# Attention with a state and top-1 experts on one Trainium2 core: first loads moved to SyncE's queue, idle products ahead of the first batch, batch 2 turned earlier, the last result stored sooner

## The chip, the cores and the metric

The kernel runs on one core of a Trainium2 chip. The metric is the device time of one execution in microseconds, the median of three runs. Besides it there is a profile of one execution: for each engine (TensorE or PE, its weight loads PEld, VectorE or DVE, ScalarE or ACT, GpSimd or POOL, and SyncE or SP, which only issues transfers) every instruction with its start and its duration. The span of the profile is the time between the first and the last instruction of the execution.

## What is computed

Two blocks, one behind the other, in float32. The first is an attention between tokens x, (8, 8, 512, 64) for batch, head, token and width, and 32 states per batch and head, in both directions. The second sends every one of the 8 x 544 rows of 512 numbers that come out to one of eight experts, the one with the largest logit.

```
scores  = softmax(0.125 * x @ state^T);  xread = scores @ state     # 512 rows per batch and head
scores2 = softmax(0.125 * state @ x^T);  sread = scores2 @ x        # 32 rows per batch and head
rows    = concat(xread, sread), heads side by side                  # (8*544, 512)
e       = argmax(rows @ w_gate);  gate = softmax(rows @ w_gate)[e]
out     = gate * (relu(rows @ w1[e]) @ w2[e])                       # w1[e] 512x1024, w2[e] 1024x512
```

## The kernel before

The 512 token rows of a batch nearly always want the same expert, so each batch is run through one expert, whose number is found from the data. The 256 rows that come from the states are sorted by expert into groups of 32 and run four groups at a time, in "rounds" of 128 rows; each row group streams its own expert's weights. Three rounds are run in the main path.

**Batches.** For batch b, `states_w1` multiplies the states by w1 once (PSUM `pG`, copied to `G`), so that the first expert layer becomes `up`: for each of eight f, one product of `G` with the attention weights `aT` (`aTe` or `aTl` in the profile) into `ph`, and a relu by ScalarE into `hT`. The second layer is `down` for batches 0 to 2 (products `py`, results `y`) and `down_by_halves` for batches 3 to 7. The latter replaces eight block products by seven (`pX`, `pD`, `pX`, `pY`, `pZ`, `pW`, `pD`, in this order), with sums made by VectorE (`Sa`, `Sb`) and GpSimd (`Ta`, `Tb`); its four results `yC`, `yD`, `yB`, `yA` (`yh` in the profile) are stored from ScalarE's queue, `yA` after the last `pD`.

**Attention.** `stages(b)` is a generator: each of its steps runs in one slot. The first step turns x (`xt`, two VectorE transposes) and the states (`stT`: a VectorE transpose into 64 partitions, and a copy to the other 64 by the engine passed in). Later steps make scores (`pc`), their transposes `sx`, the exponentials, `aT` and, for the other direction, the weights `a`, their transposes `pt` and rows `pw`, then logits (`pl`), counts (`pr`) and the choice of the expert (`eb`), which SyncE reads to address the expert's weights.

**Order.** All compute instructions keep the order in which the program writes them (the wrapper `InOrder`). Work is interleaved by hand: `up`, `down` and `down_by_halves` call `next(insert)` between products, and each call is one slot: it runs a step of `others()`, which is first the attention of later batches, then `sort_states`, then the rounds. A generator's bare `yield` lets a slot pass. Batch 0 and part of batch 1 have no earlier batch to hide beside: `begin()` writes them out, first with `up` of half of batch 0's rows (`one`), then of the other half (`two`) with steps of `beside()` between them. `first()` takes batch 1 to its end.

**Rounds.** `round_x` transposes the 128 rows (`ptx`, evicted to `sxT`), `round_up` multiplies by w1 (`pgh`), `round_h` transposes the hidden rows (`pth`), `round_down` multiplies by w2 (`pgy`) and `round_out` scales the result (`ys`, VectorE) and stores it with an indirect transfer from GpSimd. The weight tiles of the rounds (`s` in the profile, 1 MB each in four transfers of 256 KB) have S1B = 4 and S2B = 3 buffers, and `fetch` asks for the next one after each use; all of them, like the batches' weights `w1t` and `w2t`, go through SyncE's queue in the order of the program. Each transfer also waits for the one issued eight transfers before it.

PSUM has four banks in the pool `ps_p` (the function `bank`), four for `pc` while the attention lasts, and later two for `ps_t` and two for `ps_g`. In the profile, nearly all instructions have line 48, that of the wrapper, so groups are told apart by their tiles.

Of the kernel before, what the change touches and what calls it, by code (L numbers as in the profile page):

```python
# [20 lines left out]
def kernel(  # L21
# [46 lines left out]
    NFC = F // 128  # L68
# [24 lines left out]
    def load_x(b, q):  # L93
        x_nat[b] = att.tile([128, H, NC, D], FP32, tag="x", bufs=3, name="x_nat")
        for h in (slice(0, 4), slice(4, 8)):
            q.dma_start(out=x_nat[b][:, h].rearrange("p h c d -> p h (c d)"),
                        in_=x[b, h].rearrange("h (p c) d -> p h (c d)", c=NC))
# [3 lines left out]
    def load_states(b, q0, q1):  # L101

        rows = state[b].rearrange("h n d -> n h d")
        to = st2[b] = att.tile([64, H, D], FP32, tag="st", bufs=3, name="st2")
        q0.dma_start(out=to[0:32], in_=rows)
        for u in range(2):
            q1.dma_start(out=to[32:64, :, ts(u, 32)], in_=rows[:, :, ts(1 - u, 32)])
# [89 lines left out]
    def bank(name):  # L197
        return ps_p.tile([128, 512], FP32, tag="p", name=name)
# [3 lines left out]
    def turn_x(b, xt, h):  # L202
        dve.transpose(xt[:, h].rearrange("p h c u t -> p (h c u t)"),
                      x_nat[b][:, h].rearrange("p h c d -> p (h c d)"))
# [107 lines left out]
    def fetch_batch(b):  # L312
        if b < B:
            load_x(b, sp)
            load_states(b, sp, sp)
# [116 lines left out]
    def begin():  # L432

        nonlocal G, hT

        ps = bank("pss")[:, 0:4]
        for q in range(4):
            pe.matmul(ps[:, q:q + 1], lhsT=st2[0][0:32].rearrange("n h d -> n (h d)").rearrange("n (p c) -> n c p", c=4)[:, q, :],
                      rhs=ones_f[0:32], start=True, stop=True, skip_group_check=True)
        sums = att.tile([128, 4], FP32, name="sums")  # L440
        dve.tensor_copy(out=sums[:], in_=ps)
        pr = bank("prg")[0:1, 0:E]
        for q in range(4):
            pe.matmul(pr, lhsT=sums[:, q:q + 1], rhs=wg4[:, q, :], start=(q == 0), stop=(q == 3), skip_group_check=True)
        most(0, pr)
        turn_states(0, act.copy)
        xt, sx = new_xt(), new_sx()
        turn_x(0, xt, slice(0, 4))
        e = expert_of(eb, 0)
        at_once(w1_parts(0, e, 2))  # L450
        turn_x(0, xt, slice(4, 8))
        pc = new_pc()
        for g in range(2):
            scores(0, xt, pc, g)
        one, two = slice(0, 2), slice(2, 4)
        soft[0] = (sx,)
        turn_scores(pc, sx, 0)
        turn_scores(pc, sx, 1)
        less_max(sx, one, dve)
        exponential(sx, one)  # L460
        load_x(1, act)
        act.dma_start(out=wg[:], in_=moe_w_gate.rearrange("(c p) e -> p c e", p=128))
        load_states(1, act, act)
        turn_scores(pc, sx, 2)
        turn_scores(pc, sx, 3)
        over_sum(sx, one, dve)
        turn_read(0, one)
        G = states_w1(new_G(), w1s[0], stG[:, 0])
        less_max(sx, two, dve)
        exponential(sx, two)  # L470
        nm = write_max(pc)
        over_sum(sx, two, dve)
        turn_read(0, two)
        at_once(w2_parts(0, e))
        fetch_batch(2)
        for r in range(NR):
            sp.dma_start(out=ss_dram[ts(r, 128)], in_=blank[:])
        hT = new_hT()
        up(G, aT[0], hT, one)
        soft[0] += write_weights(pc, nm)  # L480
        xt, sx = new_xt(), new_sx()
        turn_x(1, xt, slice(0, 4))
        turn_x(1, xt, slice(4, 8))
        turn_states(1, act.copy)
        first_e = att.tile([1, 1], FP32, name="first_e")
        dve.tensor_copy(out=first_e[:], in_=eb[0:1, 0:1])

        def beside():
            for b in range(2):
                states_gates(b)  # L490
            pc = new_pc()
            scores(1, xt, pc, 0)
            yield

            pr = bank("pre")[:, 0:1]
            pe.matmul(pr, lhsT=ones_f[0:1].to_broadcast([1, 128]), rhs=first_e[:], start=True, stop=True)
            scores(1, xt, pc, 1)
            exps, gates = logits_x(0)
            dve.tensor_copy(out=eb[:, 0:1], in_=pr)
            for i in range(4):  # L500
                turn_scores(pc, sx, i)
            less_max(sx, ALL, dve)
            nm = write_max(pc)
            yield
            exps()
            gates()
            count(0)
            turn_write(0)
            yield
            write_rows(0)  # L510
            exponential(sx, ALL)
            soft[1] = (sx,) + write_weights(pc, nm)
            over_sum(sx, ALL, dve)
            turn_read(1)
            yield
        up(G, aT[0], hT, two, beside())

# [8 lines left out]
    def w1_parts(b, e, cols=1):  # L526

        t = w1s[b] = wpool.tile([128, NDC, F], FP32, tag="w1", name="w1t")
        rows = moe_w1[ds(e, 1)].rearrange("o (c p) f -> p (o c) f", p=128)
        f = F // cols  # L530
        return [lambda k=k: sp.dma_start(out=t[:, :, ts(k, f)], in_=rows[:, :, ts(k, f)]) for k in range(cols)] if cols > 1 else \
            [lambda k=k: sp.dma_start(out=t[:, k], in_=rows[:, k]) for k in range(NDC)]
# [6 lines left out]
    def at_once(parts):  # L539
        for p in parts:  # L540
            p()
# [9 lines left out]
    def new_G():  # L551
        return ffn.tile([128, 2, F], FP32, tag="G", name="G")

    def states_w1(G, w1t, st, halves=(0, 1), bank=bank):

        for k in halves:
            pg = [bank("pG") for _ in range(2)]
            for q in range(4):
                for g in range(2):
                    pe.matmul(pg[g][ts(q, 32), :], lhsT=st[ts(g, 64), q, :],  # L560
                              rhs=w1t[ts(g, 64), q, ts(k, 512)], start=True, stop=True, skip_group_check=True)
            for g in range(2):
                act.copy(G[:, g, ts(k, 512)], pg[g][:])
        return G
# [299 lines left out]
    def rounds(r0, r1):  # L864
        need1.extend((r, k, half) for r in range(r0, r1) for k in range(NDC) for half in range(2))
        need2.extend((r, f) for r in range(r0, r1) for f in range(NFC))
        round_experts(r0)
        fetch(2, 0)
        yield
        yield  # L870
        round_in(r0)
        fetch(S1B - 2, S2B)
        for _ in range(5):
            yield
        for r in range(r0, r1):
            round_x(r)
            if r + 1 < r1:
                round_experts(r + 1)
                round_in(r + 1)
            yield  # L880
            for k in range(NDC):
                round_up(r, k)
                fetch(2, 0)
                yield
                if k < NDC - 1 and r + 1 < r1:
                    yield
            round_relu(r)
            yield
            round_h(r)
            yield  # L890
            for f in range(0, NFC, 2):
                for i in range(2):
                    round_down(r, f + i)
                    fetch(0, 1)
                yield
                if r + 1 < r1 or f < 2:
                    yield
            round_out(r)


    begin()

    def first():

        yield
        turn_write(1)
        exps, gates = logits_x(1)
        yield
        exps()
        choose(1)  # L910
        e1 = expert_of(eb, 1)
        at_once(w1_parts(1, e1))
        lazy.extend(w2_parts(1, e1))
        gates()
        yield
        write_rows(1)
        yield
        xsT = [turn_rows(b) for b in range(2)]
        yield
        for b in range(2):  # L920
            logits_s(b, xsT[b])

    lazy = []

    def attention():

        gens, slot = [first()], 0
        while gens:
            b = 2 + slot // 4
            new = slot % 4 == 0 and b < B  # L930
            if new:
                gens.append(stages(b))
                next(gens[-1])
            for g in gens[:len(gens) - new]:
                try:
                    next(g)
                except StopIteration:
                    gens.remove(g)
            slot += 1
            yield  # L940
# [170 lines left out]
```

## Time and profile before

| | |
|---|---|
| time | 468.24 us (467.53 to 468.88, three runs) |
| profiled execution | 467.59 us, span 465.8 us |
| first TensorE product of batch 0's scores | 8.93 us |
| first product of `up`, batch 0 | 18.72 us |
| first `pg` product of batch 2 | 52.41 us |
| `pG` of batch 1 | 72.34 us |
| last TensorE product ends | 459.15 us |
| `yA` stored, issue by ScalarE | 460.10 us |
| `ys` of the last round stored, issue by GpSimd | 461.00 us |
| HBM read and written | 94.15 MB and 14.95 MB |

A line of the timeline gives the start, the duration, the engine, the source line, the operation with its tiles as out<-in, the shape and the number of instructions merged into it; in brackets stands the idle time of that engine just before, and what ended it. "issue" is time in which the engine waited for nothing that the profile shows: its sequencer was busy issuing something else. A table of windows gives, for each stretch of time, how long each engine was busy in it, the clock that TensorE was granted as a share of full speed (PEclk), the share of time the DMA engines were busy and what they moved.

### The profile page before, as it was taken

To read this page: it belongs to the slowest core of one execution; us is meant where nothing else is said; L and a number is where in the kernel's file an instruction comes from. 1 tells how busy PE (TensorE), PEld (TensorE's weight loads), DVE (VectorE), ACT (ScalarE), POOL (GpSimd) and SP (SyncE) were. 2 spreads that over 40 slices of the span, in tenths; PEclk is the share of its full clock that TensorE was granted. 3 is DMA by queue.
4 is the path that set the end of the run, shared out by engine and by line. 5 is a ranking of instruction groups with operands and counts; after the bars stand their busy time and mean duration, and the time that the engine had idled before them with its cause. 6 is when DMAs were issued, how large, how long until landed. Compare 5 with 4: busy or idle time off the path is not lost. (4 is left out here: it accounts for less than half of the span.)

```text
span 465.8 us, 9496 instructions
## 1 busy us (share of the span) xinstructions
PE 441.5 (95%) x3699; PEld 252.8 (54%) x3699; DVE 178.0 (38%) x445; ACT 120.0 (26%) x267; POOL 87.1 (19%) x75
## 2 busy tenths in 40 slices
PE   3699799999999999999999999999999999999994
PEld 3376454555455554445764476646565466537652
DVE  4827672757383652233150133213131214203221
ACT  1354133434242442323301322022203221123000
POOL 2000121214121211014223022040331022400400
PEclk9899899999999999999999999999999999999998
DMA  6593569233866442529999996999789996670691
GB/s 200 187 313 111 174 229 315 88 107 118 303 184 248 151 156 91 185 72 343 386 385 298 382 341 223 340 389 362 231 264 377 342 306 222 197 274 0 216 303 36
DMA packets 68402, 110.04 MB, mean 236 GB/s; under 512 B 12927, under 2 KB 27263, under 8 KB 68352
## 3 DMA queue, kind: packets, MB, share of 16 engines
q1 hardware_dynamic: 57696, 98.66, 62.1%
q10 hardware_dynamic: 10256, 9.67, 6.1%
q0 software_dynamic: 400, 1.05, 0.6%
q8 instruction: 31, 0.51, 0.4%
q14 instruction: 19, 0.16, 0.1%
HBM read 94.15 MB, written 14.95 MB: 234 GB/s over the span
## 5 line engine op out<-in xcount | busy, mean ns | idle before, releaser
L48 PE MATMUL py<-w2t,hT 128*128 128x512 f32 x192 | 88.5, 607 | 0.0
L48 PE MATMUL ph<-aTl,G 128*128 128x512 f32 x160 | 71.9, 598 | 0.0
L48 ACT ACTIVATE hT<-ph 128x512 f32<-128x512 f32 (+1 forms) x72 | 39.3, 551 | 118.0 <-PE ph L48 118.0
L48 PEld LDWEIGHTS py<-w2t,hT 128*128 128x128 f32 x192 | 35.2, 192 | 39.9 <-issue 39.7
L48 POOL TENSOR_TENSOR Ta<-w2t,Ta 128x1024 f32<-128x1024 f32 x10 | 24.9, 2488 | 138.0 <-PE pD L48 101.8
L48 PEld LDWEIGHTS ph<-aTl,G 128*128 128x128 f32 x160 | 29.5, 190 | 38.4 <-issue 37.4
L48 PE MATMUL ph<-aTe,G 128*128 128x256 f32 (+1 forms) x128 | 45.8, 509 | 2.6 <-ACT G L48 2.6
L48 PE MATMUL pX<-w2t,hT 128*128 128x256 f32 x160 | 36.8, 383 | 0.0
L48 PEld LDWEIGHTS pX<-w2t,hT 128*128 128x128 f32 x160 | 29.9, 190 | 10.1 <-issue 6.5
L48 PEld LDWEIGHTS ph<-aTe,G 128*128 128x128 f32 x128 | 24.5, 200 | 19.2 <-issue 12.3
L48 DVE TENSOR_TENSOR Sa<-hT 128x256 f32<-128x256 f32 x20 | 9.9, 502 | 56.7 <-ACT hT L48 56.7
L48 DVE SCALAR_TENSOR_TENSOR yh<-pY,gw,yh 128x256 f32<-128x256 f32 x20 | 8.3, 477 | 47.2 <-PE pY L48 47.2
L48 PE MATMUL pgy<-s,shT 128*32 128x512 f32 x192 | 26.1, 599 | 0.1
L48 ACT ACTIVATE yh<-pX,gw 128x256 f32<-128x256 f32 x30 | 12.1, 474 | 52.1 <-PE pX L48 52.1
L48 PE MATMUL pgh<-s,sxT 128*32 128x512 f32 x192 | 23.1, 598 | 0.0
L48 DVE STREAM_TRANSPOSE sx<-pc 128x256 f32<-128x256 f32 x32 | 11.6, 417 | 28.9 <-PE pc L48 28.9
L48 POOL TENSOR_TENSOR sx<-sx,mx 128x1024 f32<-128x1024 f32 x6 | 11.5, 1914 | 58.0 <-DVE mx L48 58.0
L48 PE MATMUL pc<-xt,stT 32*32 32x128 f32 x1024 | 18.6, 303 | 3.7 <-DVE xt L48 3.7
L48 ACT COPY G<-pG 128x512 f32<-128x512 f32 x32 | 16.8, 594 | 19.8 <-PE pG L48 17.3
L48 ACT ACTIVATE y<-py,gw 128x512 f32<-128x512 f32 x12 | 8.3, 688 | 48.4 <-PE py L48 48.4
L48 PE MATMUL pZ<-Tb,Sb 128*128 128x256 f32 x80 | 18.6, 386 | 0.0
L48 DVE STREAM_TRANSPOSE xt<-x_nat 128x1024 f32<-128x1024 f32 x16 | 18.5, 1195 | 0.0
(155 smaller groups left out, 505.4 us busy)
## 6 DMA issues: line engine op xcount, KB each, us to landing
s<-in_moe_w_dram SPq DMA_DIRECT2D x192, 256.0 KB, 5.1
w2t<-in_moe_w_dram SPq DMA_DIRECT2D x32, 512.0 KB, 6.6
w1t<-in_moe_w_dram SPq DMA_DIRECT2D x28, 512.0 KB, 6.2
x_nat<-in_x_dram SPq DMA_DIRECT2D x14, 512.0 KB, 5.1
out_dram<-yh ACTq DMA_DIRECT2D x20, 256.0 KB, 5.1
out_dram<-y ACTq DMA_DIRECT2D x12, 256.0 KB, 2.5
at_dram<-aTl SPq DMA_DIRECT2D x5, 512.0 KB, 3.6
w1t<-in_moe_w_dram SPq DMA_DIRECT2D x2, 1024.0 KB, 6.0
```

The lines of the kernel that those rows point to most:

```text
L48: ins = getattr(self.engine, name)(*args, **kw)
```

## The change

1. In `begin()`, batch 1's x, states and the gate weights are no longer issued by ScalarE in the middle of batch 0's softmax, but by SyncE right behind w1 of batch 0; w2 of batch 0 and batch 2's x and states follow there too, ahead of the batch's softmax instead of behind it.
2. Ahead of `up` of batch 0, TensorE gets seven products of the identity with itself into a bank that nobody reads, to keep it occupied while it would wait.
3. The copy of batch 1's turned states goes from ScalarE to GpSimd.
4. The first step of `stages(2)` runs inside `beside()`, after batch 1's maxima, instead of in a slot of its own; `first()` passes one slot more before batch 1's logits.
5. The rounds start one slot later and the last round's w2 products are packed into consecutive slots; each round's result is scaled and stored right after its last product, in the last round ahead of batch 7's last `pD` instead of behind it.

```diff
@@ begin()
         at_once(w1_parts(0, e, 2))
+        load_x(1, sp)
+        load_states(1, sp, sp)
+        sp.dma_start(out=wg[:], in_=moe_w_gate.rearrange("(c p) e -> p c e", p=128))
+        at_once(w2_parts(0, e))
+        fetch_batch(2)
...
         exponential(sx, one)
-        load_x(1, act)
-        act.dma_start(out=wg[:], in_=moe_w_gate.rearrange("(c p) e -> p c e", p=128))
-        load_states(1, act, act)
...
         G = states_w1(new_G(), w1s[0], stG[:, 0])
+        idle = bank("idle")
+        for _ in range(7):
+            pe.matmul(idle[:, 0:128], lhsT=ident[:], rhs=ident[:], start=True, stop=True, skip_group_check=True)
         less_max(sx, two, dve)
...
         turn_read(0, two)
-        at_once(w2_parts(0, e))
-        fetch_batch(2)
...
-        turn_states(1, act.copy)
+        turn_states(1, gp.tensor_copy)
@@ beside()
             nm = write_max(pc)
+            early.append(stages(2))
+            next(early[0])
             yield
@@ rounds()
-        for _ in range(5):
+        for _ in range(6):
             yield
...
                     fetch(0, 1)
+                if f + 2 == NFC:
+                    round_out(r)
                 yield
-                if r + 1 < r1 or f < 2:
+                if r + 1 < r1:
                     yield
-            round_out(r)
@@ first()
         turn_write(1)
+        yield
         exps, gates = logits_x(1)
@@ attention()
-                gens.append(stages(b))
-                next(gens[-1])
+                gens.append(early.pop() if early else stages(b))
+                if b > 2:
+                    next(gens[-1])
```

More of the change, by code (lines that the diff above doesn't have):

```diff
@@ L894, in rounds @@
                     fetch(0, 1)
+                if f + 2 == NFC:
+                    round_out(r)
                 yield
-                if r + 1 < r1 or f < 2:
+                if r + 1 < r1:
                     yield
-            round_out(r)
+    early, lazy = [], []
     begin()
@@ L921, in first @@
             logits_s(b, xsT[b])
-    lazy = []
     def attention():
```

## The prediction

> **What bounds the kernel now.** First the page's busy shares and its clock row, to see which engine is the limit and whether it ran at full speed.
>
> ```profile
> PE 441.5 (95%) x3699; PEld 252.8 (54%) x3699; DVE 178.0 (38%) x445; ACT 120.0 (26%) x267; POOL 87.1 (19%) x75
> PEclk9899899999999999999999999999999999999998
> ```
>
> TensorE is busy 441.5 of 465.8 us, so only its 24.3 us of idle time, and time at a low clock, can be won. The clock row dips in slices 2 and 5 (11.6 to 23.3 and 46.6 to 58.2 us; the dip at the end has no work under it). The window table in steps of 1 us dates the dips (columns: PE, PEld, DVE, ACT, POOL busy, PEclk, DMA share, GB/s):
>
> ```profile
> 18.00:19.00 1.00, 0.28 (x1) 0.28 (x2) 0.97 (x3) 0.92 (x2) 0.00 (x0) 1.00 1.08 373
> 19.00:20.00 1.00, 1.00 (x4) 0.72 (x4) 1.00 (x2) 1.00 (x3) 0.00 (x0) 0.62 1.26 204
> 22.00:23.00 1.00, 1.00 (x5) 0.85 (x4) 0.93 (x3) 0.38 (x1) 0.00 (x0) 0.67 0.00 0
> 53.00:54.00 1.00, 0.94 (x58) 0.84 (x67) 0.74 (x4) 0.36 (x3) 0.58 (x3) 0.69 0.74 294
> 56.00:57.00 1.00, 1.00 (x2) 0.34 (x1) 0.00 (x0) 0.00 (x0) 0.00 (x0) 0.60 0.00 0
> ```
>
> The clock is half from 19.24 (0.62 is 0.24 full and 0.76 half) to 22.66, and from 53.38 to 56.80: 3.4 us each, 1.7 us of work lost each time. Ahead of each lies an idle TensorE. The timeline and TensorE's waits say what each gap waited for:
>
> ```profile
> 17.58 0.71 DVE L48 STREAM_TRANSPOSE aTe<-sx 128x512 f32<-128x512 f32 x1
> 18.09 2.05 ACT L48 COPY G<-pG 128x512 f32<-128x512 f32 x4 [2.48 <-issue]
> 18.72 10.64 PE L48 MATMUL ph<-aTe,G 128*128 128x256 f32 x40 [2.65 <-ACT G L48]
> 30.50 0.54 PE L48 MATMUL pg<-wg,stT 64*32 64x8 f32 x16 [0.93 <-ACT hT L48]
> 51.60 0.66 DVE L48 STREAM_TRANSPOSE stT<-st 64x512 f32<-64x512 f32 x1
> 52.41 0.20 PE L48 MATMUL pg<-wg,stT 64*32 64x8 f32 x2 [2.19 <-DVE s L48]
> ```
>
> ScalarE stood 2.48 us issuing batch 1's loads while finished pG banks waited for it. At 52.41 batch 2's stT arrives late from VectorE, and its copy on GpSimd adds a 0.45 us wait. The chain of waits holds only the last 1.2 us, so the tail is read from the timeline:
>
> ```profile
> 451.12 4.38 PE L48 MATMUL pgy<-s,shT 128*32 128x512 f32 x16
> 455.43 3.72 PE L48 MATMUL pD<-w2t,Sa 128*128 128x256 f32 x16
> 459.98 0.74 DVE L48 TENSOR_SCALAR ys<-pgy,xg 128x512 f32<-128x512 f32 x1
> 461.00 1.00 POOL L48 DMA_INDIRECT out_dram<-ys,xg  x1 [18.84 <-DVEq L1007]
> ```
>
> The last pgy takes 4.38 us where its like take 1.92: it waits for w2 tiles (2.4 us by the waits view). Then ys comes last, after batch 7's result.
>
> **What the skill says.** "TensorE: Matmul & The Clock Gate", Part 1: activity is judged in free-running windows of about 3.4 us; an idle window halves the clock, a busy one restores it. The trace agrees: 3.42 us each, and the two dips start 34.14 us, ten windows, apart. "DMA: Bandwidth & Descriptors", Queues, rings and completion order: SyncE's and ScalarE's DMAs each own one ring on each DMA engine, consumed in ring order. So x queued behind w1 on SyncE should not take w1's bandwidth, as it could from ScalarE's ring; no two large loads overlap there before, so the trace can't confirm it. Same page, Issuing engines are not separate DMA queues: another issuer saves only issue time; that is what ScalarE's 2.48 us were.
>
> **The change part by part.**
>
> *Loads moved to SyncE.* w1's second half lands by 14.98 (its product starts there), the 1 MB of x behind it at the 390 GB/s of the trace by about 17.5, w2 by 23, x2 by 26. They are needed at 23.4 (x1, after aTe on VectorE), about 38 (w2) and 39 (x2): hidden. ScalarE's four G copies start when its exponential ends, at 15.60, and are done by 17.7. The first up product then waits for aTe, 17.58 + 0.71 = 18.29: start 18.35 for 18.72, gain 0.37 us.
>
> *Seven idle products.* They need a bank freed by the first G copy: 16.2. Each is two records of 128x128; x8 transposes of that size took 1.04 us, 0.13 each, so 14 x 0.13 = 1.8 us, to 18.0: hidden. Upper bound, the spacing of 128x256 records (3.72 / 16 = 0.23): 3.3 us, to 19.5, which would cost 1.1. I take 1.8. In the window 15.83 to 19.24 TensorE was busy 0.8 us (23%); now 0.27 + 1.8 + 0.9 = 3.0 (87%), while 12.41 to 15.83 with 61% stayed at full clock. Gain 1.71 us. Up then ends at 18.35 + 10 x 0.86 = 26.95 for 29.3.
>
> *Batch 1's stT copy on GpSimd.* There it takes 0.61 us (rows of later batches) with GpSimd idle. ScalarE's two relus follow at once: 25.7 + 1.44 for the weights = 27.16 for 30.06. TensorE's pg of batch 1 hangs on them: 2.9 us early in all to here.
>
> *Batch 2 turned early.* VectorE takes x2 and stT (2.33 + 0.66 us) at 39.7 to 42.7, before gw and the reciprocals. Behind them: s ready at 43.55 (before 43.45), so ScalarE's xs, exponential and weights stay at 43.6 to 46.4, in absolute time. TensorE, now 2.9 us early, ends its py products at 45.7 and waits about 0.3 us for the weights. aTe of batch 1 stays near 49.45; its reader pl, one yield later, comes at 52. The gap of 2.19 + 0.45 us and the second half-clock window (1.71) go, and a 0.25 us wait around pl.
>
> *first() one yield later.* Now pr, which picks batch 1's expert, stands 8 py records before pG instead of 16 plus more. In the before, w1 is issued 1.49 us after pr starts, flows from 0.9 us later; here pr starts at 57.2, issue 58.7, 2.1 MB plus a 0.26 MB store at 390 GB/s end at 65.7, landing 66.6 to 67.5. TensorE reaches pG at 57.4 + 3.6 + 1.0 + 3.6 = 65.6: a **new wait** of 1.0 (0 to 2). pG at 66.7 for 72.34: 5.6 us early.
>
> *Rounds one slot later.* ptx came after the first pG half and waited 1.0 us for a ps_t bank; now it follows the second, with ScalarE idle: about 0.7. Gain 0.3.
>
> *Last round.* Its first two w2 tiles are multiplied 3.5 us later (after the second pX, not before), the others where they were. Only three tiles are loaded ahead, so f3 to f7, 5.2 MB with 0.5 MB of stores, must flow from about 436.6: at the 320 GB/s of 440 to 454, 18 us, f7 at 455.7 for 454.4. Loss 1.3 us (0 to 3).
>
> *ys stored ahead of the last pD.* VectorE's 0.74 and the store (issue at 461.0, 3.2 us to land: 464.2) go beside pD. The last is then yA's store: issued at 460.1, 3.1 us: 463.2. Gain 1.0.
>
> Sum: 5.6 + 0.3 - 1.3 + 1.0 = 5.6 us: 468.24 - 5.6 = **462.7**.
>
> **The rivals.**
> *The clock windows fall elsewhere, or loads starve the joints (466.0).* If the timed runs' windows split the gaps, the two 1.7 us were never lost there. For it: the windows run free. Against: the profiled run took 467.6, as fast as the timed ones, with both dips. 462.7 + 3.4 = 466.1; with w1 and tail at their bad ends (1.0 + 1.7) and idle products too long, the same.
> *Nothing new waits (460.2).* w1 in time (1.0) and the tail's tiles no later than before (1.3): 462.7 - 2.3 = 460.4.
> *Slower (471).* The rounds' 48 MB now meet the batches' weights differently on one in-order queue, DMA near 380 GB/s from 209 to 326 us. If five batches each find weights 0.9 us late, w2 landing between 5.9 and 9.5 us, 4.5; if the tail's 5.7 MB flow at the page's mean 234 GB/s, 24 us for 18, 6 more: 462.7 + 10.5 = 473; at four fifths of that 471. Against: TensorE shows no weight wait from 240 to 440, and most round deadlines move later with their releases.
>
> **How the numbers follow.** Forecast 0.50, clock or joints 0.22, nothing new 0.16, slower 0.08, and 0.04 for gains and losses cancelling. Range 460.0 to 466.5 leaves out the last two. Faster 0.88, same 0.04, slower 0.08.
>
> **What would show it.** PEclk 1.00 at 19 to 23 and 53 to 57; ph starting near 18.4 with relus 0.86 apart from the first; no wait at pg of batch 2; a wait for w1 ahead of pG near 66; pgy's DMA waits at the end near 3.5 us; the last store from ScalarE's queue. Wrong if ph starts after 19.5, if pc's or pG's first products move later, or if pgh or pgy waits appear before 430.

## Result and the profile after

The changed kernel takes 462.52 us (median of five runs, 462.07 to 463.14), the kernel before, measured beside it, 468.24 us. The ratio is 0.9874 with a 95% interval of 0.9857 to 0.9892. The span of the profiled execution goes from 465.8 to 460.7 us, 5.1 us less; the other 0.6 us of the difference of the medians lies between executions (the profiled execution of the kernel before was one of its shorter ones).

The page of the changed kernel, its busy shares and its row of granted clocks:

```profile
PE 442.5 (96%) x3713; PEld 252.7 (55%) x3713; DVE 177.4 (39%) x445; ACT 119.2 (26%) x266; POOL 87.7 (19%) x76
PEclk9999999999999999999999999999999999999999
```

TensorE has 14 instructions more, the idle products, and both dips of the clock row are gone. It was not busy for 18.2 us instead of 24.3; 1.8 us of that difference are the idle products themselves. Four of the windows of 1 us at the two dips of before, the first of them just ahead of the first dip (columns: PE, PEld, DVE, ACT and POOL busy, PEclk, DMA share, GB/s):

```profile
18.00:19.00 1.00, 0.52 (x4) 0.36 (x3) 1.00 (x2) 0.00 (x0) 0.00 (x0) 1.00 0.91 220
19.00:20.00 1.00, 1.00 (x6) 0.87 (x6) 0.97 (x3) 0.04 (x1) 0.00 (x0) 1.00 1.06 386
53.00:54.00 1.00, 1.00 (x76) 0.73 (x64) 0.62 (x3) 0.00 (x0) 0.00 (x0) 1.00 1.20 330
56.00:57.00 1.00, 1.00 (x4) 0.52 (x3) 0.96 (x2) 0.00 (x0) 0.00 (x0) 1.00 0.08 20
```

At 19 to 20 us TensorE runs six products where it ran four. The timeline of the changed kernel shows what filled or closed the gaps (start, duration, engine, line, operation; in brackets the idle time ahead and what ended it):

```profile
15.85 2.03 ACT L48 COPY G<-pG 128x512 f32<-128x512 f32 x4
16.47 1.83 PE L48 MATMUL idle<-ident 128*128 128x128 f32 x14 [0.30 <-ACT G L48]
18.78 1.53 PE L48 MATMUL ph<-aTe,G 128*128 128x256 f32 x6 [0.48 <-DVE aTe L48]
28.01 0.64 PE L48 MATMUL pg<-wg,stT 64*32 64x8 f32 x16 [0.15 <-ACT hT L48]
47.69 0.35 PE L48 MATMUL pg<-wg,stT 64*32 64x8 f32 x16
```

The copies of G start at 15.85 for 18.09, the idle products fit in front of `up`, the wait of 0.93 us at batch 1's `pg` is 0.15, and batch 2's `pg` waits for nothing where it waited 2.19 and then 0.45 us.

Two joints are left in which the new kernel waits. One is batch 1's `pG`. All instructions with the tile `w1t` between 55 and 72 us (durations are minimum, median and maximum in ns):

```profile
L48 SPq DMA_DIRECT2D w1t<-in_moe_w_dram x4: 332/354/1396, 59.2 to 61.9; - x4
  DMA w1t<-in_moe_w_dram: 2.0, 3
DMA to landing us min/median/max: 5.8/6.2/6.6
```

TensorE and its weight loads sat idle 2.0 us in three pieces until w1 landed; in the kernel before the same view has no such line. `pG` took 4.00 us from its first to its last product, for 1.95 before. The four issues took from 59.20 to 62.2, because one of them took 1.4 us. That issue does not make the wait: in e7_stT_act below no issue of w1 took over 0.38 us, and the same view still gives 1.9 us. The timeline of TensorE behind it:

```profile
66.08 1.87 PE L48 MATMUL pG<-w1t,stG 64*32 64x512 f32 x12
68.17 1.91 PE L48 MATMUL pG<-w1t,stG 64*32 64x512 f32 x20 [0.22 <-DMA w1t<-in_moe_w_dram]
70.87 0.23 PE L48 MATMUL pg<-wg,stT 64*32 64x8 f32 x2 [0.16 <-ACT G L48]
71.45 0.27 PE L48 MATMUL pg<-wg,stT 64*32 64x8 f32 x14 [0.36 <-ACT G L48]
```

`pG` ends at 70.08 us instead of 74.29, 4.2 us earlier; the products next in order then wait for ScalarE's four copies of `pG`. At the next batch's `pG` (122.55 for 125.88) 3.3 us of the lead are left.

The other joint is the end, here the last round's w2 products, batch 7's last `pD` and the two last results:

```profile
448.73 2.84 PE L48 MATMUL pgy<-s,shT 128*32 128x512 f32 x16
451.50 3.72 PE L48 MATMUL pD<-w2t,Sa 128*128 128x256 f32 x16
452.69 1.00 POOL L48 DMA_INDIRECT out_dram<-ys,xg  x1 [13.91 <-DVE ys L48]
455.26 0.88 DVE L48 SCALAR_TENSOR_TENSOR yh<-pD,gw,yh 128x256 f32<-128x256 f32 x2 [2.84 <-PE pD L48]
```

The last `pD` starts 3.93 us earlier than before (455.43). The round's result is stored during it, and the last store is now `yA`, issued at 456.17. From the start of this `pD` to the end of the span it takes 9.20 us instead of 10.37. 3.93 and 1.17 make the 5.1 us.

### The profile page after: what moved, and what is told of

Same layout as the page of the kernel before. It is cut to its first block, busy times and chain, and to the rows that moved or that the text cites. A ratio compares the mean times of both kernels' runs of the same rounds, so it can differ in the third digit from the quotient of the medians.

```text
span 460.7 us, 9525 instructions
## 1 busy us (share of the span) xinstructions
PE 442.5 (96%) x3713; PEld 252.7 (55%) x3713; DVE 177.4 (39%) x445; ACT 119.2 (26%) x266; POOL 87.7 (19%) x76
## 4 chain that ended last, share of the span: by engine, by line
PE 82%; DVE 10%; DMA 3%; ACT 2%; issue 1%; SPq 1%; POOL 1%; ACTq 0%; POOLq 0%; DVEq 0%
PE ph L48 20%; PE py L48 12%; PE pD L48 8%; PE pX L48 8%; PE pgy L48 5%; PE pgh L48 5%; PE pW L48 4%; PE pY L48 4%; PE pZ L48 4%; PE pc L48 4%; PE pG L48 3%; DVE xt L48 3%; DVE sm L48 1%; PE pt L48 1%; DVE nm L48 1%; DMA w1t<-in_moe_w_dram 1%
## 5 line engine op out<-in xcount | busy, mean ns | idle before, releaser
L48 PE MATMUL py<-w2t,hT 128*128 128x512 f32 x192 | 87.5, 601 | 0.0
L48 PE MATMUL ph<-aTe,G 128*128 128x256 f32 (+1 forms) x128 | 44.0, 493 | 0.5 <-DVE aTe L48 0.5
L48 PEld LDWEIGHTS ph<-aTe,G 128*128 128x128 f32 x128 | 23.3, 190 | 15.7 <-issue 12.9
L48 ACT COPY G<-pG 128x512 f32<-128x512 f32 x32 | 16.8, 593 | 24.3 <-PE pG L48 24.3
L48 PE MATMUL pG<-w1t,stG 64*32 64x512 f32 x256 | 19.0, 605 | 1.1 <-DMA w1t<-in_moe_w_dram 1.1
L48 PE MATMUL pW<-Ta,hT 128*128 128x256 f32 x80 | 18.6, 386 | 0.0
```

Source lines behind the costliest of these rows:

```text
L48: ins = getattr(self.engine, name)(*args, **kw)
```

## Experiments

Each edit is given against the changed kernel. All were timed in five rounds beside the kernel before. The median of the latter was 468.78 us beside the first four kernels, 468.51 beside the next four and 469.06 beside the last four. Two kernels are best compared within such a group; across groups by their ratio to the kernel before, whose intervals are about 0.3% to either side.

### The first joint: idle products, loads, a copy

**Without the idle products** (e1_no_idle), and **with three instead of seven** (e8_idle3):

```
-        idle = bank("idle")
-        for _ in range(7):            # e8: range(3)
-            pe.matmul(idle[:, 0:128], lhsT=ident[:], rhs=ident[:], ...)
```

> The changed kernel without its seven idle products. Theory (they keep the granted clock up): TensorE stands idle from 16.1 to 18.8 us, the clock is half for one window of 3.4 us in the first up, and the time is about 1.7 us longer, 464.2 us. Rival (the clock would have stayed up anyway, because the loads left ScalarE's queue and the gap is shorter): no half clock between 18 and 24 us, 462.5 us, or 0.3 us less because up need not wait.

> The changed kernel with three idle products instead of seven: 0.8 us of work in a gap of 2.7 us. Theory (a window's busy share decides, and about 60% was enough in the kernel before, where 23% was not): the window around the gap is then 55 to 60% busy, so the clock stays up and the time is 462.5 us. Rival (the gap has to be filled nearly whole): a half-clock window as with none, about 464.2 us.

Measured without them: 465.61 us (463.93 to 466.88), ratio 0.9941 (0.9918 to 0.9965). Its windows:

```profile
19.00:20.00 1.00, 1.00 (x4) 0.79 (x5) 0.97 (x3) 0.00 (x0) 0.00 (x0) 0.63 0.95 314
22.00:23.00 1.00, 1.00 (x4) 0.79 (x4) 0.92 (x3) 0.38 (x1) 0.00 (x0) 0.66 0.55 197
```

The half clock is back, again for 3.4 us, and again about 1.7 us of work are lost in it. With three products the time is 462.89 us (462.26 to 463.41), ratio 0.988 (0.9855 to 0.9904), and the clock stays full, although TensorE is then busy for only 1.47 of the 3 us from 16 to 19. So the idle products are worth 2.7 us between medians of one group, and more than three of them only fill a wait. That is 1.0 us more than one window. Without them the executions spread over 3.0 us, with three over 1.2, and the mean granted clock of every timed execution says why in part: it was 0.989 to 0.998 without them and 0.996 to 0.999 with three. One window at half clock takes about 0.004 off it (half of 3.4 us in 463; a low clock behind the last product, which costs nothing, counts too). So the two fastest executions without the products, 463.93 and 464.40 us at 0.998, lost no whole window, and others may have lost more than one.

**First loads back on ScalarE, and no idle products** (e5_loads_act_no_idle):

```
-        load_x(1, sp)
-        load_states(1, sp, sp)
-        sp.dma_start(out=wg[:], ...)
-        at_once(w2_parts(0, e))
-        fetch_batch(2)
...
         exponential(sx, one)
+        load_x(1, act)
+        act.dma_start(out=wg[:], ...)
+        load_states(1, act, act)
...
         turn_read(0, two)
+        at_once(w2_parts(0, e))
+        fetch_batch(2)
```

> The changed kernel with the first loads where they were (x, gate weights and states of batch 1 from ScalarE's queue, w2 and batch 2's loads behind the softmax) and without idle products. Theory (moving the loads by itself is worth only ScalarE's issue time, 0.4 us at the start of up, and the idle products are worth 1.7): 0.4 us above the kernel without idle products, about 464.6 us. Rival (the early loads also matter later, since batch 2's x is now needed at 40 us): 466 us or more, with a wait for x on VectorE near 40 us.

Measured: 465.49 us (464.71 to 467.53), ratio 0.9932 (0.991 to 0.9954), against 465.61 of e1_no_idle: no difference that can be seen. In its trace the copies of G again stand behind the loads' issues, and `up` starts late:

```profile
18.92 2.05 ACT L48 COPY G<-pG 128x512 f32<-128x512 f32 x4 [2.48 <-issue]
19.56 2.72 PE L48 MATMUL ph<-aTe,G 128*128 128x256 f32 x6 [2.75 <-ACT G L48]
```

Its span is 0.5 us longer than that of e1_no_idle, and VectorE does not wait for batch 2's x near 40 us, as the rival had it. The move of the loads takes 2.48 us off ScalarE and at most 0.5 off the path, since `up` next waits for `aTe`. It matters in another way: idle products need a bank that a copy of G frees, so with the copies at 18.92 there would be no room for them. This is argued from the trace: loads on ScalarE with idle products were not run.

**The copy of stT back on ScalarE** (e7_stT_act):

```
-        turn_states(1, gp.tensor_copy)
+        turn_states(1, act.copy)
```

> The changed kernel with batch 1's stT copied by ScalarE as before, not by GpSimd. Theory (ScalarE's relus are on TensorE's path there, GpSimd is free): 0.6 us more ahead of the two relus that free the banks of pg, 463.1 us. Rival (what is won there is lost again at the wait for batch 1's weights near 46 us, since VectorE holds them up in absolute time): 462.5 us, with that wait 0.6 us shorter or gone.

Measured: 463.64 us (463.38 to 464.12), ratio 0.9897 (0.9873 to 0.9921), 0.75 us more than e8_idle3 beside it, with intervals that overlap. By the trace the copy is a part of the way to `pg`, which waits 0.93 us for ScalarE's relus as in the kernel before; `pc` behind it comes at 29.21 us for 28.57 after the change, and 0.4 us of these 0.64 are left at batch 3's first `pl` (103.84 for 103.41).

### The second joint: batch 2 turned early, and batch 1's pG

**Batch 2's first step and batch 1's logits where they were** (e4_turn_late), and **only the slot that first() passes taken out** (e9_no_yield):

```
-            early.append(stages(2))          # e4 only
-            next(early[0])                   # e4 only
...
         turn_write(1)
-        yield                                # e4 and e9
         exps, gates = logits_x(1)
...
-                gens.append(early.pop() if early else stages(b))   # e4 only, to the end
-                if b > 2:
-                    next(gens[-1])
+                gens.append(stages(b))
+                next(gens[-1])
```

> The changed kernel with batch 2's first step back in its own slot and batch 1's logits one slot earlier, as before. Theory (the gap of 2.6 us at batch 2's pg and the half clock behind it return, while the new wait for w1, 2 us in the changed kernel's trace, and the wait for G's copies, 0.7, go away): 4.6 minus 2.7 is 1.9 us more, 464.4 us, with PEclk at one half for 3.4 us near 50 to 55 us. Rival (only the prediction's own terms, 1.0 us of wait for w1): 465.5 us. Second rival (the gap is shorter than a clock window allows for when it comes 2.4 us earlier, so the clock stays up): 462.7 us.

> The changed kernel without the extra slot ahead of batch 1's logits, all else kept. Theory (the slot is needed, since pl reads batch 1's aT, which VectorE finishes near 50 us, and TensorE would stand from 47.7 to 50.1 us): 2.4 us of wait and with luck the half clock, but w1 is asked for one slot earlier and its 2.0 us wait goes: 462.9 us with the clock up, 464.6 us with it down. Rival (the wait at pl is the whole story): 465 to 466.6 us.

Measured: e4_turn_late 465.16 us (463.73 to 465.73), ratio 0.9908 (0.9875 to 0.9942); e9_no_yield 464.73 us (462.84 to 466.11), ratio 0.9901 (0.9866 to 0.9936). First TensorE's gap and two windows of e4_turn_late, then the gap of e9_no_yield:

```profile
49.99 0.24 PE L48 MATMUL pg<-wg,stT 64*32 64x8 f32 x2 [2.19 <-DVE s L48]
50.00:51.00 1.00, 0.60 (x30) 0.48 (x42) 0.88 (x5) 0.00 (x0) 0.88 (x3) 0.50 1.06 411
56.00:57.00 1.00, 1.00 (x3) 0.44 (x2) 0.00 (x0) 0.00 (x0) 0.00 (x0) 0.69 0.00 0
```

```profile
50.70 1.08 PE L48 MATMUL pl<-aTe,gst 128*32 128x128 f32 x16 [2.50 <-DVE s L48]
```

In e4_turn_late the old wait is back, and in both kernels the clock is half from 49.8 to 56.6 us, two windows and not one. In both the wait for w1 is gone, and `pG` comes at 71.10 (e4_turn_late) and 71.66 us (e9_no_yield) instead of 66.08, with a second piece at 68.17. So the early turn alone removes one wait and makes another: `pl` then stands ahead of its data, and waits 2.50 us. Only with the extra slot in `first()` is the gap closed. Of what was expected, the median of e9_no_yield came out on the side of its case with the low clock. Both cases occur among its executions: the fastest took 462.84 us with a mean clock of 0.998, which is in the range of the changed kernel, the profiled one 466.11 with 0.991. By that, most of what the slot in `first()` saves would be the clock, since the wait at `pl` that it removes is not much longer than the wait for w1 that it makes; but one execution is little to go by.

**Batch 1's pG one slot later** (e6_pg_later):

```
-            if c == (1 if b else 2) and b + 1 < B:
+            if c == 1 and b and b + 1 < B:
                 G = states_w1(new_G(), w1s[b + 1], stG[:, b + 1])
             yield
+            if c == 2 and not b:
+                G = states_w1(new_G(), w1s[b + 1], stG[:, b + 1])
```

> The changed kernel with batch 1's pG one slot later (behind the slot that follows row block 2 of batch 0's down, not ahead of it). Theory (pG waits 2.0 us for w1, and pxs and pg behind it wait 0.7 us for the copies of G; 2 us of other TensorE work ahead of it and py products behind it hide both): 2.5 us less, 460.0 us. Rival (w1's transfer is asked for by a chain that hangs on TensorE's earlier products, and something else of that slot then waits, VectorE's or GpSimd's copies for pg): 462.0 to 462.5 us.

Measured: 461.23 us (460.38 to 461.91), ratio 0.983 (0.9798 to 0.9862). In that trace the last `pD` began 2.34 us earlier than after the change (449.16), but the span was only 1.1 us shorter. So it was run once more beside the changed kernel itself (r1_after_again, r2_pg_later_again) and with three idle products (c1_pg_later_idle3):

> The changed kernel itself once more, beside the next three on one chip, so that they can be compared with it directly. Expected 462.5 us.

> e6_pg_later once more. In its first profile the last pD started 2.34 us earlier than after the change (449.16 for 451.50), but the span was only 1.1 us shorter: the last store took 4.0 us from issue to landing where it had taken 2.8. If that slow store belongs to the kernel, the span is 459.6 again and the time 461.2. If it was this one execution, the store takes 2.8 us, the span is 458.4 and the time, which is a median over many executions, stays at 461.2 or goes to 460.2.

> Batch 1's pG one slot later and three idle products instead of seven: the two findings together. Theory: idle products beyond the third only fill a wait, so the time is that of pG later alone (461.2). Rival: with fewer of them the clock window is met in fewer executions, and the median is up to 1.5 us higher and the spread over 2 us.

Measured: the changed kernel 463.35 us (462.46 to 464.17), ratio 0.9889 (0.9862 to 0.9916); pG later 460.07 us (459.45 to 461.8), ratio 0.9827 (0.98 to 0.9854); with three idle products 460.53 us (459.34 to 460.9), ratio 0.983 (0.9805 to 0.9856). TensorE in r2_pg_later_again:

```profile
66.76 0.27 PE L48 MATMUL pg<-wg,stT 64*32 64x8 f32 x14 [0.49 <-ACT y L48]
67.96 1.95 PE L48 MATMUL pG<-w1t,stG 64*32 64x512 f32 x32
```

The slot with `pxs`, `pg` and `pc` runs while w1 is on its way, and `pG` comes at 67.96 with all four parts of w1 there and no wait. The waits for copies of `pG` are gone as well; one of 0.49 us for a result takes their place. `up` starts 0.7 us earlier in this execution than in the trace of the change, which is the spread of the start. Counted from `up`, batch 3's first `pl` comes 82.5 us later here and 84.6 after the change: 2.1 us are the edit's. Between medians of the group it is 3.3 us, with intervals that allow 1 to 5. The last store, 4.0 us in the first profile, took 2.8 us in the second, so the slow one was that execution's. Three idle products do as well as seven here too. pG later is the better version: it is faster than the kernel before by 1.7%, where the change was by 1.1 to 1.3%.

### The tail

**The rounds as before** (e2_tail_old), and **the same slots but the result scaled and stored right after its last product** (e3b_store_early_pace_old):

```
-        for _ in range(6):                # both: range(5)
...
-                if f + 2 == NFC:          # e2 only
-                    round_out(r)
                 yield
-                if r + 1 < r1:            # both
+                if r + 1 < r1 or f < 2:
                     yield
+            round_out(r)                  # e2 only
```

> The changed kernel with the rounds as before: start one slot earlier, last w2 products spread, ys scaled and stored behind the last pD. Theory by the traces (the store ahead of pD is worth 1.2 us, fewer waits for w2 tiles at the end 0.5, ptx 0.2): 1.9 us more, 464.4 us. Rival by the prediction's terms (store 1.0 and ptx 0.3 gained, tiles 1.3 lost): no change, 462.5 us.

> The rounds' slots as in the kernel before, but each result scaled and stored right after its last product: the store alone. Theory from e2_tail_old (whose pD began at 451.38 for 451.50): where the rounds' slots lie is worth nothing, so this is as fast as the whole change, 462.5. Rival: the packed slots are what lets the store come early, so at least 0.5 us are lost: 463.0 or more.

Measured: e2_tail_old 463.41 us (462.96 to 464.4), ratio 0.9879 (0.9847 to 0.9911); e3b_store_early_pace_old 462.72 us (462.08 to 463.67), ratio 0.9872 (0.9846 to 0.9897), beside 463.35 for the change itself. The end of e2_tail_old:

```profile
455.94 0.74 DVE L48 TENSOR_SCALAR ys<-pgy,xg 128x512 f32<-128x512 f32 x1
456.95 0.99 POOL L48 DMA_INDIRECT out_dram<-ys,xg  x1 [17.93 <-DVEq L1014]
```

and of e3b_store_early_pace_old:

```profile
452.25 3.72 PE L48 MATMUL pD<-w2t,Sa 128*128 128x256 f32 x16
453.45 1.00 POOL L48 DMA_INDIRECT out_dram<-ys,xg  x1 [13.89 <-DVE ys L48]
```

With the old slots and the old store the last `pD` starts at 451.38, no later than after the change (451.50), and the span ends 10.5 us behind it (461.9). With the store early it ends 9.65 us behind it in e3b_store_early_pace_old (span 461.9 as well, since its `pD` starts later) and 9.2 in the change and in its second profile. So the store ahead of `pD` is worth about 0.9 to 1.3 us by the traces, and the packed slots nothing that shows. The medians alone, with their intervals, don't separate the three tails.

## Why the prediction came out as it did

The forecast was 462.7 us, the time is 462.52, but that it came so close is in part luck. Two terms of its sum were off and made up for each other: the gain up to batch 1's `pG`, 5.6 us, of which 3.3 were left a batch later, and the loss in the last round, 1.3 us, where 0.6 were gained in the first profile and nothing in the second. The medians also differ by 0.6 us more than the spans of the two traces.

**Loads, idle products, the clock: as worked out.** The copies of G follow the exponential at once (15.85 for 15.60), 14 records took 1.83 us for 1.8, and `up` starts at 18.78, not 18.35, behind `aTe`, which is 0.3 us late with the whole start of this execution: VectorE's first turn of the states began 0.28 us later than before. The prediction left open whether x, queued behind w1 on SyncE's ring, takes bandwidth from it. The two halves of w1 took 5.1 and 7.2 us from issue to landing, 4.9 and 7.1 before, so it took little if anything. `up` of the first half, which took 10.6 us in the kernel before, takes 8.9, the 1.7 us of one window at half clock. The length that "TensorE: Matmul & The Clock Gate", Part 1 of the Trainium skill, gives for the free-running windows, about 3.4 us, agrees with all traces here: each half-clock stretch was 3.4 us, or 6.8.

**Batch 1's first scores: 2.4 us early, not 2.9.** `pc` comes at 28.57 for 30.97. The late start took 0.3 to 0.4 of it.

**Batch 2 turned early: as worked out.** `pt` waits 0.23 us for the weights (0.3 was said), `pg` nothing. e4_turn_late and e9_no_yield show that the early turn needs the slot: the old place of both leaves a gap of 2.19 us, the early turn without the slot one of 2.50. The slot without the early turn was not run.

**The wait for w1: the step that was too small.** The step put the first issue at 58.7, the flow at 390 GB/s and the wait at 1.0 (0 to 2). The issue came at 59.20, but TensorE was late by as much (66.08 for 65.6), so the time from the one to the other was as said. The flow was not: from 60 to 68 us the windows of 2 us show 231, 285, 377 and 404 GB/s, 324 on average, with the DMA engines busy for 93 to 102%. The wait was 2.0 us, the end of the range given, and it was 1.9 to 2.4 in the seven other traces with the same order of products here (the second of the changed kernel, and e1, e2, e3b, e5, e7 and e8). Why the engines moved so little at 60 to 64 us is not shown. **Not in the sum at all** were the waits behind `pG`: `pxs` and `pg` follow it at once in the order of the program and need banks that ScalarE's 2 us of copies free. They cost about 0.8 us: `pxs` took 0.70 us for 0.38, and `pg` waited 0.16 and 0.36. So 5.6 us at this point were 4.2 at the end of `pG` and 3.3 a batch later. e6_pg_later and its repetition confirm both: one slot later, both kinds of wait are gone but for 0.2 us in the first of the two traces, and about 2.1 us come back.

**The last round: the step that was too large.** It forecast the last w2 tiles 1.3 us late, and they were not. Two of its numbers don't hold. It read 320 GB/s for 440 to 454 us, where the windows give 280 at a busy share of 0.86. And 18 us from 436.6 are 454.6, not 455.7: for the 1.1 us between it names nothing, and without them the loss would be 0.2. (The 2.4 us of the waits view, too, are four waits in three groups of `pgy`, 1.6 of them in the last.) The windows of the kernel before and then of the changed one, same columns as above:

```profile
438.00:442.00 4.00, 4.00 (x27) 2.05 (x26) 2.30 (x5) 0.00 (x0) 2.24 (x1) 1.00 0.74 234
442.00:446.00 4.00, 4.00 (x26) 2.75 (x27) 2.29 (x7) 0.00 (x0) 0.16 (x1) 1.00 0.87 315
```

```profile
438.00:442.00 4.00, 4.00 (x19) 2.55 (x16) 2.07 (x4) 0.00 (x0) 0.78 (x1) 1.00 1.07 399
442.00:446.00 4.00, 4.00 (x25) 2.00 (x24) 1.66 (x4) 0.00 (x0) 0.00 (x0) 1.00 1.00 364
```

Before, SyncE issued no tile from 435.8 to 440.7 us, and the engines were busy for 74% and 87% of these stretches: the rate was in part that at which products freed buffers for the next issues. With the products packed, the changed kernel moved 326 GB/s from 433.1 to 450.5 (321 in the second profile), about the same stretch of the program 3.5 us earlier, where the kernel before moved 278 from 436.6 to 454.4. So 320 was about right for the change, though it isn't what was read. The 399 and 364 are not rates to count on: the second profile shows 340 and 344 in the same two windows, and the kernel before moved 291 from 446 to 450 with its engines fully busy. The last three groups of `pgy`, 1.92 us each where nothing disturbs them, took 2.48 us more than that together (3.07 in the second profile), before 3.04, and with the old slots 2.14 in e2_tail_old and 2.42 in e3b_store_early_pace_old: no loss by the new slots, and no gain from them either.

**The early store: as worked out**, 1.17 us for 1.0.

In sum, by the traces: 3.3 us a batch after the second joint, 0.2 at `ptx` (waits 0.73 for 0.96), 0.6 in the waits of `pgy` in this execution, 1.2 at the end, less 0.2 that the traces don't place: 5.1. Of the rivals, the one with clock windows elsewhere did not occur in the traces: the dips were in every trace that had the gaps. The mean clocks of the other executions say more. In all 39 of the kernel before beside the experiments it was 0.985 to 0.993, with 0.990 in the trace, so each lost about as much clock as two windows take (0.007) or more, a low clock behind the last product included. In the fastest of e1_no_idle and e9_no_yield, with 0.998, the windows did fall so that none was lost. The other half of that rival, w1 at its bad end, came true. Nothing came in the direction of the slower one: no product shows a wait for a weight between 80 and 430 us, and the weight loads waited 1.8 us there for the rounds' tiles, 1.4 before. (The 380 GB/s that this rival read from 209 to 326 us are 344 by the windows.)

## What to carry to other kernels

When a change closes several gaps in a row, work out for each transfer whose issue hangs on the path how much of its flight is left to hide: the lead won at one joint is spent at the next one, and moving one independent slot of work ahead of the product that waits was worth about 2 us here, two fifths of what the whole change gained in the traces. A transfer rate read from a stretch in which the DMA engines are not fully busy may be the rate of its feeding; look at the busy share beside the GB/s before it is put into a sum. A full share gives no fixed rate either: it went here with anything from 231 to 404 GB/s, so a wait that hangs on it needs a range. And a short idle stretch of TensorE costs more than its own length if it fills most of a clock window: a few products that nobody reads, placed where TensorE would wait anyway, took the loss away here and delayed nothing that shows.

## What the runs showed of the hardware

- A clock window need not be idle throughout to be followed by half clock. By the windows of the profile, TensorE was busy for these shares of the 3.42 us ahead of a half-clock stretch: 20% in e5_loads_act_no_idle, 23% at both dips of the kernel before, 32% in e1_no_idle, 39% in e4_turn_late and 44% in e9_no_yield. The clock stayed up after 61% (kernel before, 12.41 to 15.83 us), and in e8_idle3, where three products of the identity, 0.94 us, made every such stretch between 13 and 22 us at least 55% busy; seven products were not needed. The gaps in the windows that lost it were 2.2 to 2.8 us long. Where between 44 and 55% the border lies, or whether another measure than busy time decides, was not measured.
- One busy window did not always bring the clock back. In the kernel before, the half-clock windows were busy throughout (19.24 to 22.66 us, and 53.38 to 56.80), and full clock followed. In e4_turn_late and e9_no_yield the first, 49.78 to 53.20 us, was busy for 82 and 73% by the records, and a second followed, busy throughout, before the clock returned. About 1.9 us of the first one in e4_turn_late were products on parts of the array, 64 x 32 and 32 x 32. The part of the Trainium skill named above says that an idle window halves the clock and a busy one restores it; these shares are what was seen here, and what counts as busy stays open.
- Executions whose first 20 us hold the same work on the path differ by up to 1 us there (the first `pG` product at 12.11 us and `up` at 17.80 in c1_pg_later_idle3, 12.94 and 18.78 after the change), so traces are compared best from a common event on, not from the start.
